# A value projection of 128x512 issued as two column halves of 128x256

## The chip, the core and the metric

The kernel runs on one core of a Trainium2 chip. The metric is device time in microseconds of one launch, as the median of several runs; beside it stands one execution that the hardware profiler recorded, with a span from its first to its last instruction. Engines are named as in the profile: PE is TensorE's matmul, PEld its weight load, DVE VectorE, ACT ScalarE, POOL GpSimd, SP the queue that issues most transfers.

## What is computed

The input x has 2048 rows of 512. A gate g = sigmoid(x . gate_w) mixes two branches per row:

```python
def _A_ref(x, wqkv, w_phi, wo):          # 32 heads of 16
    q, k, v = ...                        # x @ wqkv, split by head
    pq = einsum("bhsd,hdf->bhsf", q, w_phi)
    pk = einsum("bhsd,hdf->bhsf", k, w_phi)
    phi_q = concatenate([softmax(pq), softmax(-pq)], -1)
    phi_k = concatenate([softmax(pk), softmax(-pk)], -1)
    kv = einsum("bhsf,bhsd->bhfd", phi_k, v)
    z  = einsum("bhsf->bhf", phi_k)
    o = einsum("bhqf,bhfd->bhqd", phi_q, kv) / (einsum("bhqf,bhf->bhq", phi_q, z)[..., None] + 1e-6)
    return o @ wo
def _B_ref(x, w1, b1, w2, b2):           # 512 -> 1792 -> 512
    r = relu(x @ w1 + b1)
    return (r * r) @ w2 + b2
g = sigmoid((x * gate_w).sum(-1))
return g * A + (1 - g) * B
```

## The kernel before

**Precision.** Nearly every large product is made of three. A float32 array is split by `split` into a rounded part (type float32r, name ending in `h`) and a remainder (`l`). `mm3(o, a, b, sa, sb, first, last)` then adds high x high, high x low and low x high into the same PSUM tile. Its three lines are L69, L70 and L71 of the kernel before. Each matmul has a weight load of its own in the profile: the operand `a[:, sa]`, 128x128, is loaded into the array, and `b[:, sb]` is streamed through it.

**Tiling.** The rows are cut into 4 blocks of 512 (`NB`), each into 4 chunks of 128 (`NC`), so that there are 16 chunks. The 512 inputs are cut into 4 slices of 128 (`NK`).

**The branches.** The dense branch runs through a `work_list` of 2 sweeps x 4 blocks x 7 slices of the hidden layer: an "up" product (tile `u`, 12 matmuls of 128x512), ReLU and square on ACT, a split, and a "down" product into four PSUM tiles `d`. Two up products run ahead of the down products. The attention branch is laid over it by a table of slots: `at(slot, f, ...)` puts a step between two entries of the work list. For each chunk in the first sweep:

- `do_k` makes the keys' product `k` (a `project` of 12 matmuls) and its exponentials on DVE and ACT.
- `do_v` makes the values' product `v`, again `project(c, st["x", b], st["wb"], "v")`: the stationary operand is a slice of x, the streamed one the whole 512 columns of the split weights `wvh`, `wvl`. ACT then copies `v` out of PSUM into `vext`, which keeps a column of ones beside each head's 16 values.
- `do_kv`, for every second chunk, adds 2 x 32 small products of the exponentials with `vext` into `kvps`.

After the first sweep `kv_done` (DVE copies on L433, two transposes `kvt` on PE) lays the sums out, and the second sweep's slots hold the queries' products `q`, the numerators `num`, and the output projection `att`.

**Order.** The Tile framework turns the program text into one instruction stream per engine. It orders by priority, and `tc.high_priority(offset=AHEAD)` lifts a step ahead by `AHEAD` = 150 in program order. So more instructions in the text can move others. `k`, `v` and other short-lived products come from two one-bank pools by `bank(name)`. During the first sweep's attention work only one of these is in rotation, the other holds `kvps`.

The small matrices for the folded key and query weights (`fold`, L143) are float32 products, not float32r: tile `foldk`, 128x128.

Of the kernel before, what the change touches and what calls it, by code (L numbers as in the profile page):

```python
# [16 lines left out]
P = 128  # L17
S, D, H, DH, F = 2048, 512, 32, 16, 1792
NK = D // P
# [13 lines left out]
def tile_gated_mix(ctx: ExitStack, tc: tile.TileContext, xT, xn, wqT, wkT, wphi, wv, wo, w1, b1, w2, b2, gw, out):  # L33
    nc = tc.nc
# [16 lines left out]
    def bank(name):  # L51
        p = banks[taken[0] % len(banks)]
        taken[0] += 1
        return p.tile([P, 512], F32, tag="s", name=name)
# [11 lines left out]

    def mm3(o, a, b, sa, sb, first, last):
        (ah, al), (bh, bl) = a, b
        nc.tensor.matmul(o, ah[:, sa], bh[:, sb], start=first, stop=False)  # L69
        nc.tensor.matmul(o, ah[:, sa], bl[:, sb], start=False, stop=False)  # L70
        return nc.tensor.matmul(o, al[:, sa], bh[:, sb], start=False, stop=last)  # L71

    ALL = slice(0, 512)
    halves = (slice(0, 256), slice(256, 512))
# [7 lines left out]
    def row():  # L82
        return work.tile([P, D], F32, tag="row", name="row", bufs=6)
# [26 lines left out]
    st, up_w, down_w = {}, {}, {}  # L110
# [74 lines left out]
    def project(c, xs, ws, nm):  # L185
        ps = bank(nm)
        sc = slice(c * P, (c + 1) * P)
        for k in range(NK):
            mm3(ps, xs[k], ws[k], sc, ALL, k == 0, k == NK - 1)
        return ps  # L190
# [100 lines left out]
    def attended(o, u, wos):  # L291
        ps = bank("att")
        for r in range(2):
            for t in range(2):
                mm3(ps, o[r], wos[2 * r + t], slice((2 * t + u) * P, (2 * t + u + 1) * P), ALL,
                    r + t == 0, r + t == 2)
        return ps


    def up_step(ps, k, xs, wf):  # L300
        st["up"] = mm3(ps, wf, xs[k], slice(k * P, (k + 1) * P), ALL, k == 0, k == NK - 1)
# [104 lines left out]
        st["phi", n] = scaled(e3, r, nc.gpsimd)  # L406

    def do_v(b, n, c):
        ps = project(c, st["x", b], st["wb"], "v")
        with tc.high_priority(offset=AHEAD):  # L410
            nc.scalar.activation(heads(vext[n % NV])[:, :, :DH], ps.rearrange("p (h f) -> p h f", f=DH), AF.Copy)

# [68 lines left out]
    for b in range(NB):  # L481
        for c in range(NC):
            s = b * SL + 3 * c - 3 if b else 7 + c
            at(s, gate_load, b * NC + c)
            at(s + 3, gate_chunk, b * NC + c)
        at(b * SL + 4, do_x, b + 1)
        for c in range(NC):
            n = b * NC + c
            s = 5 + 2.9 * n
            at(s, do_k, b, c)  # L490
            at(s + 2, do_v, b, n, c)
            if c % 2:
                at(s + 5, do_kv, n - 1)
# [23 lines left out]
    hid, last = {}, len(work_list) - 1  # L517
# [19 lines left out]
    for t, (sw, b, i) in enumerate(work_list):  # L537
# [14 lines left out]
        for c in range(NC):  # L552
            n = b * NC + c
            done = ("f", n) in st
            if sw == 0:
                o = row()
                nc.scalar.activation(o, b2b, AF.Copy, scale=rest[:, n:n + 1])
            else:
# [3 lines left out]
                o = st["f", n]  # L562
# [53 lines left out]
```

## Time and profile before

| | |
|---|---|
| median of 3 runs | 531.95 us (530.74 to 532.16) |
| profiled execution, span | 528.2 us |
| around the span (median less span) | 3.75 us |
| PE busy | 519.0 us, 98% of the span, 3475 matmuls |
| PEld busy | 417.6 us, 79%, 3475 loads |
| DVE / ACT / POOL busy | 356.5 / 234.1 / 77.0 us |
| matmuls into `v` | 192, from 40.9 us to about 256 us |

For the profiled execution the profile gives the span and no other time. The 3.75 us are what the runs' median has beyond it. Matmul durations in the profile are modelled and overlap: a 128x512 product shows 389 ns, while the next one starts about 227 ns after it. What a product costs PE is therefore read from the distance of starts, not from its duration or from the busy sum.

### The profile page before, as it was taken

Reading aid. Unit: us, or ns where it says so; the run is one execution under the profiler, and the core shown is the slowest. Engines: PE = TensorE matmul, PEld = TensorE weight load, DVE = VectorE, ACT = ScalarE, POOL = GpSimd, SP = SyncE. Lnnn points to the kernel's source line nnn. Section 1 sums busy time; section 2 is a strip of 40 time slices with the busy share of each in tenths; the row PEclk is TensorE's granted clock in tenths of the full one; section 3 lists DMA queues with packets and bytes.
Section 4 is the critical chain, followed back from the end, with each engine's and each line's share of the span. In section 5 each row is a group of like instructions: output and inputs, shape, how many; then the busy total and the mean of one; then the engine's idle time right before and its main releaser. Section 6 shows DMA issues by size and latency. Waiting matters only on the chain.

```text
span 528.2 us, 8945 instructions
## 1 busy us (share of the span) xinstructions
PE 519.0 (98%) x3475; PEld 417.6 (79%) x3475; DVE 356.5 (68%) x608; ACT 234.1 (44%) x404; POOL 77.0 (15%) x61
## 2 busy tenths in 40 slices
PE   8998999999999999999999999999999999999997
PEld 4876888888888888888878878787887878787785
DVE  4688546833656334566769897998878887779423
ACT  4874424623335234354644663463435353535230
POOL 2001111111111111011103121102011111112000
PEclk9999999999999999999999999999999999999999
DMA  7974004200032000434346114134102311022102
GB/s 255 297 234 131 1 1 161 81 2 1 24 138 79 2 0 22 159 85 137 81 146 215 34 40 124 66 107 130 45 17 89 113 49 30 24 77 94 47 1 79
DMA packets 30834, 45.16 MB, mean 86 GB/s; under 512 B 5704, under 2 KB 12360, under 8 KB 30792
## 3 DMA queue, kind: packets, MB, share of 16 engines
q1 hardware_dynamic: 30328, 44.20, 26.8%
q8 instruction: 27, 0.44, 0.4%
q10 hardware_dynamic: 432, 0.39, 0.2%
q14 instruction: 15, 0.12, 0.1%
q0 software_dynamic: 32, 0.01, 0.0%
HBM read 29.89 MB, written 8.39 MB: 72 GB/s over the span
## 4 chain that ended last, share of the span: by engine, by line
PE 63%; DVE 15%; DMA 7%; ACT 5%; SPq 5%; issue 2%; POOL 2%; DVEq 0%; POOLq 0%; ACTq 0%
PE u L69 6%; PE u L71 6%; PE u L70 6%; PE d L71 6%; PE d L70 6%; PE d L69 6%; SPq L259 4%; PE k L69 3%; PE v L69 2%; PE k L70 2%; PE k L71 2%; PE v L70 2%; PE v L71 2%; DMA in<-in_w 2%; PE att L69 2%
## 5 line engine op out<-in xcount | busy, mean ns | idle before, releaser
L305 ACT ACTIVATE r<-u,b1c 128x512 f32<-128x512 f32 x56 | 38.5, 687 | 152.1 <-PE u L71 143.5
L69 PE MATMUL d<-w2h,hh 128*128 128x512 f32 x224 | 87.5, 390 | 0.0
L69 PE MATMUL u<-xh,w1h 128*128 128x512 f32 x220 | 86.8, 395 | 0.4 <-ACT w1h L61 0.4
L70 PE MATMUL d<-w2l,hh 128*128 128x512 f32 x224 | 87.2, 389 | 0.0
L71 PE MATMUL d<-w2h,hl 128*128 128x512 f32 x224 | 87.2, 389 | 0.0
L71 PE MATMUL u<-xh,w1l 128*128 128x512 f32 x220 | 85.8, 390 | 0.1
L70 PE MATMUL u<-xl,w1h 128*128 128x512 f32 x220 | 85.7, 390 | 0.0
L64 DVE TENSOR_TENSOR hl<-r,hh 128x512 fp32r<-128x512 f32 x56 | 42.8, 764 | 55.9 <-ACT hh L61 55.9
L233 POOL TENSOR_TENSOR ez<-e,z 128x512 f32<-128x512 f32 x32 | 41.4, 1316 | 187.7 <-ACT e L205 187.7
L214 POOL TENSOR_TENSOR e<-e,r 128x1024 f32<-128x1024 f32 x16 | 32.4, 2025 | 202.1 <-DVE r L210 144.8
L208 DVE TENSOR_REDUCE sm<-e 128x64 f32<-128x1024 f32 x32 | 39.0, 1217 | 28.5 <-ACT e L205 28.3
L69 PEld LDWEIGHTS u<-xh,w1h 128*128 128x128 f32 x220 | 41.3, 188 | 12.2 <-ACT hh L61 1.6
L71 PEld LDWEIGHTS d<-w2h,hl 128*128 128x128 f32 x224 | 42.1, 188 | 8.7
L69 PEld LDWEIGHTS d<-w2h,hh 128*128 128x128 f32 x224 | 42.0, 188 | 8.7
L70 PEld LDWEIGHTS d<-w2l,hh 128*128 128x128 f32 x224 | 42.1, 188 | 8.6
L71 PEld LDWEIGHTS u<-xh,w1l 128*128 128x128 f32 x220 | 41.3, 188 | 9.1 <-DVE w1l L64 0.6
L70 PEld LDWEIGHTS u<-xl,w1h 128*128 128x128 f32 x220 | 41.3, 188 | 8.2
L205 ACT ACTIVATE e<-e 128x1024 f32<-128x1024 f32 x32 | 33.8, 1055 | 23.2 <-DVE e L203 22.4
L257 ACT ACTIVATE phiT<-tb 32x256 f32<-32x256 f32 x64 | 26.4, 413 | 34.6 <-DVE tb L251 33.9
L61 ACT ACTIVATE hh<-r 128x512 fp32r<-128x512 f32 x56 | 35.2, 628 | 1.3
L306 ACT ACTIVATE r<-r 128x512 f32<-128x512 f32 x56 | 35.1, 627 | 1.0
L566 DVE SCALAR_TENSOR_TENSOR row<-d,rest,row 128x512 f32<-128x512 f32 (+1 forms) x33 | 22.4, 731 | 8.5 <-PE d L71 8.5
(106 smaller groups left out, 875.4 us busy)
## 6 DMA issues: line engine op xcount, KB each, us to landing
in<-in_xT SPq DMA_DIRECT2D x32, 256.0 KB, 3.8
in<-in_w SPq DMA_DIRECT2D x24, 256.0 KB, 3.1
phiT<-tb SPq DMA_DIRECT2D x192, 32.0 KB, 1.8
row<-in_xn SPq DMA_DIRECT2D x16, 256.0 KB, 2.8
part<-row SPq DMA_DIRECT2D x16, 256.0 KB, 2.0
row<-part SPq DMA_DIRECT2D x16, 256.0 KB, 3.7
out<-row SPq DMA_DIRECT2D x15, 256.0 KB, 2.3
row<-in_wkT SPq DMA_DIRECT2D x4, 256.0 KB, 5.8
```

Of the source, the lines that this page charges most:

```text
L61: i = nc.scalar.activation(hi, src, AF.Copy)
L64: elo.tensor_tensor(lo, src, hi.bitcast(F32), ALU.subtract)
L69: nc.tensor.matmul(o, ah[:, sa], bh[:, sb], start=first, stop=False)
L70: nc.tensor.matmul(o, ah[:, sa], bl[:, sb], start=False, stop=False)
L71: return nc.tensor.matmul(o, al[:, sa], bh[:, sb], start=False, stop=last)
L205: nc.scalar.activation(ef, ef, AF.Exp)
L208: nc.vector.tensor_reduce(sm, e3, AX.X, ALU.add)
L214: eng.tensor_tensor(e3, e3, w.unsqueeze(2).to_broadcast([P, 2 * H, DH]), ALU.mult)
L233: nc.gpsimd.tensor_tensor(ez[:, hs, :], e3[:, hs, :], zbc[half], ALU.mult)
L257: nc.scalar.activation(dst, src, AF.Copy)
L305: nc.scalar.activation(r, ps, AF.Relu, bias=b1c[:, fc:fc + 1])
L306: nc.scalar.activation(r, r, AF.Square)
```

## The change

The values' product of a chunk is no longer one group of 12 matmuls over 512 columns. It is two groups of 12 over 256 columns each, one after the other, into the two halves of the same PSUM tile. `start` is set only on the first matmul of the first half, `stop` on the last slice of each half. The stationary slices of x are the same in both halves, and are loaded once for each matmul as before. ACT's copy of `v` still follows the whole tile. `skip_group_check` is an argument of the build and not an instruction.

```diff
     def mm3(o, a, b, sa, sb, first, last):
         (ah, al), (bh, bl) = a, b
-        nc.tensor.matmul(o, ah[:, sa], bh[:, sb], start=first, stop=False)
-        nc.tensor.matmul(o, ah[:, sa], bl[:, sb], start=False, stop=False)
-        return nc.tensor.matmul(o, al[:, sa], bh[:, sb], start=False, stop=last)
+        skip = o.shape[-1] < 512
+        nc.tensor.matmul(o, ah[:, sa], bh[:, sb], start=first, stop=False, skip_group_check=skip)
+        nc.tensor.matmul(o, ah[:, sa], bl[:, sb], start=False, stop=False, skip_group_check=skip)
+        return nc.tensor.matmul(o, al[:, sa], bh[:, sb], start=False, stop=last, skip_group_check=skip)
...
     def do_v(b, n, c):
-        ps = project(c, st["x", b], st["wb"], "v")
+        ps = bank("v")
+        sc = slice(c * P, (c + 1) * P)
+        for h in halves:
+            for k in range(NK):
+                mm3(ps[:, h], st["x", b][k], st["wb"][k], sc, h, k == 0 and h is halves[0], k == NK - 1)
```

`halves` is `(slice(0, 256), slice(256, 512))`. The two instruction streams differ as follows. First, on PE at the first values' product, before: the last slices of `v`, and then the down products `d`.

```order
L69 MATMUL v<-wvh_293,xh_2_164 128x512
L70 MATMUL v<-wvl_294,xh_2_164 128x512
L71 MATMUL v<-wvh_293,xl_2_165 128x512
L69 MATMUL v<-wvh_299,xh_3_173 128x512
L70 MATMUL v<-wvl_300,xh_3_173 128x512
L71 MATMUL v<-wvh_299,xl_3_174 128x512
L69 MATMUL d_303<-w2h_245,hh 128x512
```

The same place on PE after the change: the end of the first half and the beginning of the second.

```order
L70 MATMUL v<-wvh_293,xh_2_164 128x256
L71 MATMUL v<-wvl_294,xh_2_164 128x256
L72 MATMUL v<-wvh_293,xl_2_165 128x256
L70 MATMUL v<-wvh_299,xh_3_173 128x256
L71 MATMUL v<-wvl_300,xh_3_173 128x256
L72 MATMUL v<-wvh_299,xl_3_174 128x256
L70 MATMUL v<-wvh_281,xh_0_136 128x256
L71 MATMUL v<-wvl_282,xh_0_136 128x256
L72 MATMUL v<-wvh_281,xl_0_137 128x256
```

All four slices of x are gone through twice; the 16 places hold 384 matmuls of 128x256 where there were 192 of 128x512. Apart from these, one matmul changes its place on PE. It is the first of an up product near the end of the first sweep, where `kvt` transposes the summed values. The piece of the difference, by names without numbers of buffers and lines:

```diff
 MATMUL d<-w2h,hl 128x512
-MATMUL u<-xh,w1h 128x512
 MATMUL kvt<-ident,row 128x128 x2
 MATMUL q<-wqh,xh 128x512
 ...
 MATMUL q<-wqh,xl 128x512
+MATMUL u<-xh,w1h 128x512
 MATMUL u<-xl,w1h 128x512
```

It moves from ahead of the two transposes to behind the twelve query products. On ACT one pair changes places, a little earlier. Before, the ReLU stands ahead of the third split of the output weights:

```order
L411 ACTIVATE vext_108<-v 128x32x16
L61 ACTIVATE wqh_2603<-foldq_2598 128x512
L305 ACTIVATE r<-u,b1c 128x512
L61 ACTIVATE woh_2795<-in 128x512
L61 ACTIVATE wqh_2651<-foldq_2646 128x512
```

On ACT after the change, the split comes first:

```order
L416 ACTIVATE vext_108<-v 128x32x16
L61 ACTIVATE wqh_2795<-foldq_2790 128x512
L61 ACTIVATE woh_2987<-in 128x512
L306 ACTIVATE r<-u,b1c 128x512
L61 ACTIVATE wqh_2843<-foldq_2838 128x512
```

The ReLU now stands behind a split that waits for transfers of `wo`. On DVE one small `rest<-gate` operation of 128x1 moves ahead of four others; POOL and SP keep their order.

## The prediction

> **What bounds the kernel now.** I read the page's busy shares first, then PE's waits, then the starts of single matmuls in the timeline.
>
> ```profile
> span 528.2 us, 8945 instructions
> PE 519.0 (98%) x3475; PEld 417.6 (79%) x3475; DVE 356.5 (68%) x608; ACT 234.1 (44%) x404; POOL 77.0 (15%) x61
> PEclk9999999999999999999999999999999999999999
> ```
>
> PE has work for 98% of the span, at the full granted clock in every slice. A busy share of overlapping matmuls proves little, so the waits of PE come next: who it waited for, total us, times, longest.
>
> ```profile
> PE warm L360 <- DVE zeros L354: 1.2, 1, 1.2
> PE k L69 <- ACT vext L411: 1.1, 1, 1.1
> PE num L270 <- DMA phiT<-tb: 1.1, 2, 0.6
> PE u L69 <- ACT w1h L61: 0.4, 1, 0.4
> PE kvt L444 <- DVE row L433: 0.4, 1, 0.4
> PE v L69 <- DVE e L203: 0.3, 1, 0.3
> PE foldk L143 <- DVE wkl L64: 0.2, 1, 0.2
> ```
>
> All seven together make 4.7 us. So the span is the sum of what PE's instructions cost each other in distance, and a change of that distance goes into the time nearly whole. No slack in PE can swallow more than a part of the 1.4 us that `k` and `v` wait in the table above. The values' products are 192 in the stretch from 40 to 256 us (a window of the tile `v` alone; PE's busy time and count come first after the length):
>
> ```profile
> 40.00:256.00 216.00, 47.13 (x192) 35.35 (x192) 9.15 (x16) 1.00 0.20 62
> ```
>
> What one of them costs is seen in the timeline of PE at a values' product in the middle (start, duration):
>
> ```profile
> 154.16 0.50 PE L69 MATMUL v<-wvh,xh 128*128 128x512 f32 x1
> 154.50 0.40 PE L70 MATMUL v<-wvl,xh 128*128 128x512 f32 x1
> 154.74 0.39 PE L71 MATMUL v<-wvh,xl 128*128 128x512 f32 x1
> ...
> 157.01 0.39 PE L69 MATMUL u<-xh,w1h 128*128 128x512 f32 x1
> ```
>
> From 154.74, the third of twelve, to 157.01, where the next group starts, there are ten distances: 2.27 us, or 0.227 us each. The shown duration of 0.39 is latency. The 192 products thus cost 192 x 0.227 = 43.6 us. The first distance is longer, 0.34 us, and the weight loads of the same place say why:
>
> ```profile
> 154.16 0.19 PEld L69 LDWEIGHTS v<-wvh,xh 128*128 128x128 f32 x1
> 154.27 0.19 PEld L70 LDWEIGHTS v<-wvl,xh 128*128 128x128 f32 x1
> 154.50 0.19 PEld L71 LDWEIGHTS v<-wvh,xl 128*128 128x128 f32 x1
> ```
>
> After the small products the first load has nothing to hide behind. 0.34 - 0.227 = 0.11 us is the price of a bare load, which the next load's start, 0.11 later, confirms. In the steady run a load starts with the product before it and is done long before 0.227 is over. This is the margin that a half-width product uses up.
>
> **The change part by part.** Removed: 192 products of 512 columns. Added: 384 of 256 columns with 384 loads of 128x128 in place of 192. The columns streamed are the same in number. What remains is whether a half-width product follows after half of 0.227, that is 0.1133 us, or later. No float32r product of 256 columns is in the trace, so I bound it.
>
> From below: the float32 products of the folded weights, on full 128x128 weights of the same size, with a load each. The timeline shows sixteen in a row, and the tile's summary their duration:
>
> ```profile
> 22.46 1.95 PE L143 MATMUL foldk<-row 128*128 128x128 f32 x16
> ...
> L143 PE MATMUL foldk<-row x32: 270/275/377, 22.5 to 29.4; 128*128 128x128 f32 x32
> ```
>
> (1.95 - 0.275) / 15 = 0.1117 us each. Two rows of other widths tell that a float32 column costs about two of float32r:
>
> ```profile
> L270 PE MATMUL num<-phiT,kvb 64*32 64x256 f32 x256 | 10.6, 382 | 1.2 <-DMA phiT<-tb 1.1
> L223 PE MATMUL kvps<-e,vext 128*17 128x32 f32 x1024 | 10.3, 197 | 0.0
> ```
>
> (382 - 197) / (256 - 32) = 0.83 ns of latency per column, against 0.227 / 512 = 0.44 ns per float32r column. So 128 float32 columns are about as much streaming as 256 here, and the load is equal. This is the nearest row: 384 x (0.1117 - 0.1133) = -0.6 us.
>
> Toward the expensive side: a part of the 0.227 may be paid per product and not per column. The warm-up products at the start, also 512 columns, show it. Their first and last regular loads, nine rows:
>
> ```profile
> 1.60 0.15 PEld L360 LDWEIGHTS <-zeros 128*128 128x128 bf16 x1 [0.27 <-issue]
> ...
> 5.01 0.15 PEld L360 LDWEIGHTS <-zeros 128*128 128x128 bf16 x1 [0.27 <-issue]
> ```
>
> 3.41 / 8 = 0.426 us each, 1.88 times 0.227. If the array runs at half speed there (my assumption, since the granted clock's row shows 9 from the first slice), then streaming 512 columns at full speed takes 0.213 us, and 0.0137 us of the 0.227 are a fixed part. A half-width product then costs 0.1065 + 0.0137 = 0.120 us, and 384 x 0.120 - 192 x 0.227 = +2.6 us. The load, 0.11, still fits under 0.120, but only just.
>
> The Trainium skill, TensorE: Matmul & The Clock Gate, section Back-to-back issue gap, gives the distance as columns / 1.2 ns when cold and columns / 2.4 + 2.5 ns when warm. The cold figure, 427 ns, agrees with 0.426; the warm one, 216 ns, does not agree with 0.227, so 11 ns here are not in that formula. By the page's fixed part alone the sum would be 192 x 2.5 ns = +0.5 us.
>
> The upper bound: the load cannot begin before the fixed part is over. Then a half-width product costs 0.111 + 0.0137 = 0.1247 us, and the sum is 384 x 0.1247 - 43.6 = +4.3 us. I take 0.120: the warm-up and the float32r products are 512 columns on full weights both, while the fold has the slower float32 columns, in whose pauses a fixed part can hide.
>
> The moved up product. It stood in a gap that PE has anyway:
>
> ```profile
> 270.32 0.39 PE L71 MATMUL d<-w2h,hl 128*128 128x512 f32 x1
> 270.55 0.39 PE L69 MATMUL u<-xh,w1h 128*128 128x512 f32 x1
> 271.33 0.41 PE L444 MATMUL kvt<-ident,row 128*128 128x128 f32 x2 [0.40 <-DVE row L433]
> ```
>
> `kvt` waits for DVE's copies, whose chain hangs on the last `kvps` and is not moved against PE. With the up product behind the query products, PE waits 0.227 us longer there and pays the product later: +0.2 us, its whole price, from nothing to 0.23.
>
> The swapped ReLU on ACT:
>
> ```profile
> 259.23 0.69 ACT L305 ACTIVATE r<-u,b1c 128x512 f32<-128x512 f32 x1 [1.02 <-PE u L71]
> 259.81 0.62 ACT L61 ACTIVATE woh<-in 128x512 fp32r<-128x512 f32 x1
> ...
> 267.69 0.50 PE L69 MATMUL d<-w2h,hh 128*128 128x512 f32 x1
> ```
>
> Before the ReLU ACT sat idle for 1.02 us, in which the split can run if its data has come; if not, the hidden tile is late by 0.6 us or somewhat more. The down product that uses such a tile runs at 267.69, eight microseconds on. I cost it at nothing; without that cover it would be 0.6. `vext` is copied as before, after the whole of `v`, and who waits for it moves with it. The sum: +2.6 + 0.2 = +2.8 us on the profiled 528.2, and the same on the median, which lies 3.75 above that span: 531.95 + 2.8 = 534.8.
>
> **The rivals.** *Half the columns, half the time.* The 0.227 is all per column, or the fixed part is small; the fold's pace speaks for it, the 1.88 of the warm-up against it. Price -0.6 to +0.5 us, with the moved product 531.5 to 532.7: not slower. It decides from the distance of two starts inside `v`: a slowdown over 0.3% (1.6 us, about what a measurement here can tell from no change) less the 0.2 needs 0.1133 + 1.4 / 384 = 0.117 us or more. The page's formula lies inside this rival. Chance 0.26.
>
> *The load becomes the limit.* A load, the swap and then the product, each waiting for the other: 0.1247 us, 531.95 + 4.3 + 0.2 = 536.5. For it: a bare load costs 0.11, as much as a half's streaming. Against it: the fold runs loads of the same size at 0.1117. Chance 0.10.
>
> *Nothing of the load is hidden, or the float32r rate is lost at 256 columns.* With bare loads 192 more of 0.11 cost +21 us: 553. At the pace of float32, 0.83 ns per column, 256 columns cost 0.21 and the sum is +37 us: 569. The steady 0.227 against the bare 0.34 speaks against the first; nothing in the trace against the second but that width plays no part in any row. Together 0.02. The same page, section The mechanism of Part 3, says that a load overlaps running products only where its rows of the array differ; by that rule the steady distance before would be 0.34, and the trace refutes it.
>
> *Faster by over 0.3%.* 384 products would have to follow at 0.109 or less, below the quickest row, or the order's small moves save a wait: 0.04. That the change does nothing is excluded by the streams, which hold 384 products of 128x256.
>
> **How the numbers follow.** Fixed part: 0.58, 534.8. Load-limited 0.10 and the two dear cases 0.02, all slower: 0.70. Halved cost 0.26, all within 0.3%. Faster 0.04. The range goes from the halved case at the fold's pace, 531.5, less 0.4 for the runs' spread, 531.1, to the load-limited one, 536.5, and 0.7 (half the 1.4 us between the runs before) above it, 537.2. It leaves out the dear cases and most of the faster one.
>
> **What would show it.** In the timeline of the changed kernel the starts inside `v` stand 0.120 us apart if I am right, 0.112 to 0.114 if halving is free, 0.125 if the load limits; each 0.01 is 3.8 us. Starts of `u` and `d` stay at 0.227. PE's busy sum would rise whatever happens, since durations overlap more, and proves nothing. `kvt` should wait 0.6 in place of 0.4. A new large wait of PE for `vext`, or for hidden tiles about 265 us, would make my covers wrong; distances of 0.117 or less, or the order's moves costing over 1 us, the forecast.

## The result, and the profile after

The changed kernel takes 535.5 us (median of 3 runs, 534.44 to 536.0) against 531.95: ratio 1.0073, 95% interval 1.0045 to 1.0101. That is slower by 2.4 to 5.4 us. The forecast was 534.8 in a range of 531.1 to 537.2.

The profiled execution is 533.7 us long, 5.5 us more than that of before. These are the page's first lines for the changed kernel, and the two rows of its queues that matter below:

```profile
span 533.7 us, 9329 instructions
PE 522.4 (98%) x3667; PEld 428.4 (80%) x3667; DVE 357.0 (67%) x608; ACT 233.8 (44%) x404; POOL 76.6 (14%) x61
...
q1 hardware_dynamic: 30328, 44.20, 26.2%
q8 instruction: 29, 0.48, 0.4%
```

There are 192 more matmuls and 192 more weight loads. Queue q1 moves the same 44.20 MB, but the instruction queue has 29 packets where before it had 27. Inside `v`, PE's timeline (start, duration) reads:

```profile
155.21 0.39 PE L70 MATMUL v<-wvh,xh 128*128 128x256 f32 x1
155.43 0.28 PE L71 MATMUL v<-wvl,xh 128*128 128x256 f32 x1
155.55 0.29 PE L72 MATMUL v<-wvh,xl 128*128 128x256 f32 x1
...
158.06 0.28 PE L72 MATMUL v<-wvh,xl 128*128 128x256 f32 x1
158.18 0.40 PE L70 MATMUL u<-xh,w1h 128*128 128x512 f32 x1
```

From the second product, at 155.43, to the next group, at 158.18, there are 23 distances: 2.75 us, 0.1196 us each. The first distance is longer by a bare load, as before: 0.22 in place of 0.12.

PE's waits (total us, times, longest) and the row of the transposes show what the forecast had and what it did not have:

```profile
PE num L271 <- DMA phiT<-tb: 2.5, 2, 1.6
...
PE k L70 <- ACT vext L416: 0.9, 1, 0.9
...
PE kvt L449 <- DVE row L438: 0.6, 1, 0.6
...
273.49 0.41 PE L449 MATMUL kvt<-ident,row 128*128 128x128 f32 x2 [0.59 <-DVE row L438]
```

`kvt` waits 0.6 in place of 0.4, as forecast. But the numerators, which need the transposed `phiT`, wait 2.5 us in place of 1.1. Behind the last of these waits PE ran slowly for a while:

```profile
507.10 0.63 PE L71 MATMUL u<-xl,w1h 128*128 128x512 f32 x1
507.52 0.63 PE L72 MATMUL u<-xh,w1l 128*128 128x512 f32 x1
507.95 0.63 PE L70 MATMUL u<-xh,w1h 128*128 128x512 f32 x1
```

These up products stand 0.42 to 0.43 us apart, not 0.227. Windows show the granted clock (the number after PE's, PEld's, DVE's, ACT's and POOL's times), 0.84 over 11 us there and 1.00 at the like place before:

```profile
500.00:511.00 11.00, 9.39 (x60) 6.48 (x59) 2.30 (x4) 1.28 (x3) 0.00 (x0) 0.84 0.08 22
```

From 506 to 509 us alone it is 0.50.

So the loss in this execution has three parts. By the transposes `kvt`, which start at 273.49 in place of 271.33, 2.2 us are lost. The moved up product then adds 0.2. About 3 us come from the numerators' waits (1.4 us longer than before) and the slow stretch (0.16 x 11 = 1.8 us). The experiments ask whether the last part is chance, and if not, what it is.

### The profile page after: what moved, and what is told of

Same layout as the page of the kernel before. It is cut to its first block, busy times and chain, and to the rows that moved or that the text cites. A ratio compares the mean times of both kernels' runs of the same rounds, so it can differ in the third digit from the quotient of the medians.

```text
span 533.7 us, 9329 instructions
## 1 busy us (share of the span) xinstructions
PE 522.4 (98%) x3667; PEld 428.4 (80%) x3667; DVE 357.0 (67%) x608; ACT 233.8 (44%) x404; POOL 76.6 (14%) x61
## 3 DMA queue, kind: packets, MB, share of 16 engines
q1 hardware_dynamic: 30328, 44.20, 26.2%
## 4 chain that ended last, share of the span: by engine, by line
PE 71%; DVE 11%; SPq 6%; DMA 4%; ACT 4%; POOL 2%; issue 2%; DVEq 0%; ACTq 0%; POOLq 0%
PE u L70 7%; PE d L71 7%; PE d L72 7%; PE u L72 7%; PE d L70 7%; PE u L71 7%; SPq L260 5%; PE v L70 3%; PE v L72 3%; PE v L71 3%; PE k L70 3%; PE k L71 3%; PE k L72 3%; PE att L70 2%; POOL ez L234 2%; PE att L71 2%
## 5 line engine op out<-in xcount | busy, mean ns | idle before, releaser
L64 DVE TENSOR_TENSOR hl<-r,hh 128x512 fp32r<-128x512 f32 x56 | 41.4, 739 | 57.9 <-ACT hh L61 57.9
L70 PE MATMUL v<-wvh,xh 128*128 128x256 f32 x128 | 37.0, 289 | 0.5 <-DVE e L204 0.5
L72 PE MATMUL v<-wvh,xl 128*128 128x256 f32 x128 | 36.3, 283 | 0.0
L71 PE MATMUL v<-wvl,xh 128*128 128x256 f32 x128 | 36.3, 283 | 0.0
```

What stands on the lines that cost most here:

```text
L64: elo.tensor_tensor(lo, src, hi.bitcast(F32), ALU.subtract)
```

## Experiments

**The kernel before, again.** No edit.

> The kernel before, unchanged, against itself. It tells how far its profile's waits vary: the changed kernel's profile has, beside starts 0.120 us apart inside v, a wait of the last numerators for phiT of 1.6 us (0.6 before) and up products 0.43 apart behind it, at a lower granted clock; together some 2.5 us that are not in the forecast. Theory A (the extra at the end is chance, and belongs to both kernels): here too some executions have the long wait and the slow up products; ratio 1.000, within 0.2%; spans spread by 1 to 2.5 us. Theory B (the change lengthens that wait): the last wait for phiT stays at about 0.6 us here, the tail keeps full clock, spans agree within 0.5 us.

Ratio 1.0008 (0.9998 to 1.0017); spans of single executions from 528.9 to 530.9, a spread of 2.0 us, as theory A had it. But the long wait that theory A expected is not in the one execution that was profiled. The wait for `phiT` is the one known from before:

```profile
PE num L270 <- DMA phiT<-tb: 1.1, 2, 0.6
```

It also shows that an execution takes 1.8 us more than its span (531.97 and 530.2 here). The 528.2 that the prediction was worked out on was thus a quick execution, and the 3.75 us "around the span" were half that.

**The changed kernel, again.** No edit.

> The changed kernel again, in more rounds. Theory A: the lasting part is the 384 products at 0.120 us (+2.6) and the moved up product (+0.2), so the ratio settles near 1.0053 (1.004 to 1.0065), and the tail's wait and clock differ from execution to execution. Theory B (the tail's wait belongs to the change): ratio 1.007 to 1.010, with a long last wait for phiT and a slow stretch of PE behind it again.

536.69 us, ratio 1.0111 (1.0093 to 1.013), above the ranges of both theories. Theory A falls: the extra belongs to the change. The waits for `phiT` are long again, 1.7 at the last numerators, and 2.2 at the first, which the profile puts down to ACT:

```profile
PE num L271 <- ACT xh L61: 2.2, 1, 2.2
PE num L271 <- DMA phiT<-tb: 1.7, 1, 1.7
```

**The moved up product alone.** On the kernel before:

```diff
+            if "q_first" in st and k == 0:
+                with tc.issue_after(st.pop("q_first").ins):
+                    up_step(ps, k, xs, wf)
...
+            if "q_down" in st:
+                held.enter_context(tc.issue_after(st["q_down"].ins))
```

Both names hold the last matmul of the first query product, so that neither an up nor a down product slips in ahead of it. But for the width of `v`, PE's order is then that of the changed kernel. The pairs exchanged on ACT and DVE stay as before.

> The kernel before with whole 512-column values' products, and on PE exactly the order of the changed kernel: the first matmul of one up product stands behind the first twelve query products instead of ahead of kvt. Theory A: kvt waits 0.6 us instead of 0.4, all else alike: +0.2 us, ratio 1.0004 (0.999 to 1.002). Theory B in the form that the moved order delays the queries' chain and so the numerators: a wait for phiT longer by 0.5 to 1.5 us, ratio 1.002 to 1.005.

530.89 us, ratio 1.0 (0.999 to 1.0009). `kvt` waits 0.6 and the numerators 1.1:

```profile
PE num L273 <- DMA phiT<-tb: 1.1, 2, 0.6
...
PE kvt L457 <- DVE row L446: 0.6, 1, 0.6
```

PE's order is not what lengthens the numerators' waits. What is left of the change is the number and width of PE's instructions and the pairs exchanged on ACT and DVE, so I followed the transfers that the numerators wait for.

**What is late at the last numerators.** Each pair of chunks needs 24 small transfers `phiT<-tb`, issued one after another by SP. SP's timeline for the last pair, from four profiles (before, before again, the changed kernel, the changed kernel again), each row with its start and length:

```profile
484.62 15.08 SPq L259 DMA_DIRECT2D phiT<-tb  x24
```

```profile
486.64 15.07 SPq L259 DMA_DIRECT2D phiT<-tb  x24
```

```profile
487.55 16.07 SPq L260 DMA_DIRECT2D phiT<-tb  x24
```

```profile
489.75 16.17 SPq L260 DMA_DIRECT2D phiT<-tb  x24
```

A median issue takes 0.589 us. The changed kernel's train of issues is 1.0 to 1.1 us longer, and all of it is in one issue:

```profile
490.64 1.58 SPq L260 DMA_DIRECT2D phiT<-tb  x1
```

In a window from 490.4 to 492.4 us of the same kernel, the queues show what else moved then (packets, MB, share of the 16 engines):

```profile
q1 hardware_dynamic: 96, 0.07, 13.4%
q8 instruction: 1, 0.02, 3.5%
```

One packet of instructions, 16 KB. Over the train of before, from 484.62 to 499.7, there is none:

```profile
q1 hardware_dynamic: 1056, 0.72, 17.9%
```

The same holds for the first pair's train: one instruction packet from 296.5 to 311.7 in the changed kernel, none from 294.1 to 309.3 before. So theory P: a block of program loaded while SP issues makes that issue about 1 us longer. Its rival Q: the half-width products or the order lengthen the waits themselves. The kernel before was spared at the two trains for which PE waits, and the added instructions moved later blocks onto them. The Trainium skill, Runtime: NRT & Kernel Launch, section Instruction fetch mechanics, says that each engine's program is refilled in blocks of 16 KiB, 256 instructions, by a DMA queue of its own. The 16 KB packets agree. By the Trainium skill's 256 instructions in a block, 384 added instructions are an estimated one and a half blocks, so the phase moves by half a block. The same section of the Trainium skill calls the cost of a block's boundary mostly hidden. Here it is not hidden where the packet meets an issue of SP: that issue is 1 us longer.

**The changed kernel with the program's phase moved.**

```diff
-        idle(11)
+        idle(9)
+        for i in range(52):
+            j = 32 * (i % 4)
+            nc.tensor.matmul(st["warm"][j:j + 32, :32], st["zeros"][:, j:j + 32], st["zeros"][:, :32],
+                             start=True, stop=True, skip_group_check=True)
```

Two of the eleven warm-up products give way to 52 tiny ones, which makes 50 pairs of load and matmul more. The profile shows two moves beside that, both near the start: one matmul of an up product stands eight places later on PE, and one pair on ACT changes places.

> The changed kernel with 50 more pairs of load and matmul at the very start: 2 of the 11 warm-up products are replaced by 52 tiny ones of 32x32. All else, products and order, is the same. Theory P (phase of PE's instruction loads): the 384 additional PE instructions of the change moved the later loads of PE's program onto SP's phiT issues (loads at 305.8 and 490.7 us in the changed kernel's profile, inside the trains of issues at 296.5 and 487.6), each making one issue 0.4 to 1.1 us longer; 50 pairs move these loads about 11 us earlier, to about 294 and 480, ahead of both trains. Expected: the waits of num for phiT back at about 1.1 us in total, no slow stretch of PE in the tail, and 2 to 2.7 us faster than the changed kernel: ratio to the kernel before 1.004 to 1.0065. Rival Q (the longer waits come from the 256-column products or the moved order themselves): waits of 2.5 to 3.9 us stay, ratio 1.009 to 1.013.

532.69 us, ratio 1.0041 (1.0024 to 1.0059). The numerators wait 1.1 us again, and the last train has 24 issues in 15.07 us, as in the kernel before (15.08 and 15.07):

```profile
PE num L271 <- DMA phiT<-tb: 1.1, 2, 0.6
```

```profile
488.30 15.07 SPq L260 DMA_DIRECT2D phiT<-tb  x24
```

The two packets now come at 295.4 and 486.1 us, ahead of the trains that start at 297.7 and 488.3; the second moved by 4.6 us only, not by the 11 that I expected. All 384 half-width products, the moved product and the exchanged pairs on ACT and DVE are still there, so none of them makes the long waits. P has what it asked for, Q has not.

**The same addition on the kernel before.** The same edit, with the same small moves near the start.

> The kernel before, 512 columns and old order, with the same 50 additional pairs at the start. Theory P: its loads of PE's program, at 288.9 and 480.8 us before and 312.5 and 502.4 behind the two trains of phiT issues (294.1 to 309, 484.6 to 499.7), move about 11 us earlier, so that those behind land inside both trains, near 301 and 491. Expected: the waits of num for phiT grow from 1.1 to 2.5 to 3.5 us and the kernel is slower by 1 to 2.7 us: ratio 1.002 to 1.005. Rival Q: no change, ratio 1.000 within 0.1%, waits stay at 1.1.

530.49 us, ratio 1.0005 (0.9989 to 1.002). On the total P missed: I expected 1.002 to 1.005. Only one of the two trains was hit, the last:

```profile
PE num L270 <- DMA phiT<-tb: 1.8, 2, 1.3
```

```profile
484.00 15.80 SPq L259 DMA_DIRECT2D phiT<-tb  x24
```

```profile
q8 instruction: 1, 0.02, 0.4%
```

(The last row is the window from 484 to 499.8 us.) The train is 0.7 us longer with one instruction packet in it, and PE's last wait grew from 0.6 to 1.3. The first train had none: the block there moved by 1.5 us only, not by the 11 that I had reckoned, so 50 pairs do not move all blocks alike. The 0.7 us were offset in this profile by as much at the beginning, where waits for the first transfers differ from one execution to the next. Within the interval the total shows nothing, so this run carries the mechanism in its trace and not in its time.

**Both side by side.** The changed kernel and its shifted form had run on different chips so far, so both ran on one chip:

> The changed kernel once more, on the same chip and in the same call as the shifted one (e10), since the two were compared on different chips before. Theory P: instruction loads again inside the trains of phiT issues, waits of num at 2.5 to 3.9 us, ratio 1.009 to 1.012. If the chip made the difference, this comes out near e10, at 1.004 to 1.006.

> The changed kernel with the 50 additional pairs at the start, beside e9. Theory P: waits of num at 1.1 us, ratio 1.004 to 1.006, 2 to 3.5 us under e9. If the chip made the difference, both have the same ratio within 0.2%.

The changed kernel: 534.8 us, ratio 1.0077 (1.0055 to 1.0099). The shifted one: 532.39 us, ratio 1.0027 (1.0016 to 1.0038). Both ratios lie below the ranges expected for them, 1.009 to 1.012 and 1.004 to 1.006. Their difference, 2.4 us, is within the 2 to 3.5 expected. The intervals do not touch, so it is not the chip. The waits and the last train, first of the changed kernel and then of the shifted one:

```profile
PE num L271 <- DMA phiT<-tb: 2.7, 2, 1.8
...
489.38 16.25 SPq L260 DMA_DIRECT2D phiT<-tb  x24
```

```profile
PE num L271 <- DMA phiT<-tb: 1.0, 2, 0.6
...
486.88 15.07 SPq L260 DMA_DIRECT2D phiT<-tb  x24
```

The waits make 1.7 of the 2.4 us. The rest is not shown to come from the packets: the two profiles also differ ahead of the first `v`, which starts at 42.6 and at 40.7 us. This start varies from 40.3 to 42.9 among all ten profiles of the table below, so it may be chance, or the work of the altered warm-up.

**All profiles side by side.** Two stretches of PE's timeline leave that beginning out: from the first to the last start in `v`, and from the start of `kvt` to the end of the span. The table includes the kernel with paired halves, which is described below.

| kernels | `v` | `kvt` to the end | waits of `num` |
|---|---|---|---|
| before; again; order alone | 214.4; 214.4; 214.5 | 256.9; 256.9; 257.1 | 1.1 each |
| changed and shifted; beside | 216.6; 216.7 | 257.1; 257.1 | 1.1; 1.0 |
| before, shifted (one train hit) | 214.3 | 257.7 | 1.8 |
| changed; again; beside; paired halves (both trains hit) | 216.8; 217.0; 216.9; 216.7 | 260.2; 260.0; 258.8; 258.9 | 2.5; 3.9; 2.7; 2.8 |

So `v` costs 2.1 to 2.7 us more wherever it is cut in halves, the moved product 0.2, and the hit trains 1.6 to 3.1 more in the second stretch. Of these ten profiles' twenty trains that PE waits for, nine hold an instruction packet, and each of the nine has one issue of 1.0 to 1.8 us. In the other eleven no issue is longer than 0.65. In the changed kernel run again the first numerators go on 2.1 us behind the end of their train, in its other profiles 1.4; what made these 0.8 us (2.14 less 1.38) is open.

**What sets the distance of 0.120 us.** Three kernels vary the pieces of `v`.

Four pieces of 128 columns (`h = slice(128 * i, 128 * i + 128)` for four `i`):

> The values' products in four pieces of 128 columns: 768 matmuls. If the fixed part of 0.0137 us per product is all there is, starts inside v are 0.053 + 0.0137 = 0.067 us apart and the whole costs 51.5 us against 43.6: +8 us, about 540. If a weight load of 0.11 us per product must fit between two starts, they are 0.111 to 0.114 apart, 85 to 88 us: +42 to +44 us, about 575. If load and fixed part add, 0.125 apart and +52 us.

589.32 us in one run. The timeline, from the second product of a group on:

```profile
154.77 0.27 PE L71 MATMUL v<-wvl,xh 128*128 128x128 f32 x1
...
156.67 0.28 PE L70 MATMUL v<-wvh,xh 128*128 128x128 f32 x1
```

17 distances in 1.90 us, 0.1118 each: the weight load sets the pace, as with the folds' 0.1117. `v` costs 768 x 0.1118 - 192 x 0.227 = +42 us, as the second theory said. The rest of the 58 is in waits and in the clock: `k` waits 11.0 us for ACT's `vext`, which I did not expect and did not follow up, and the mean granted clock was 0.991, which over 587.5 us is an estimated 5 us at most.

Pieces of 384 and of 128 columns (`for h in (slice(0, 384), slice(384, 512))`):

> The values' products in pieces of 384 and of 128 columns. With a fixed part of 0.0137 us per product, starts inside the wide piece are 0.160 + 0.0137 = 0.1737 us apart; if the 0.227 were all per column, 0.170. Inside the narrow piece the load sets 0.111 to 0.112, as with four pieces of 128. A pair then costs 0.285 in place of 0.240 for halves: +11 us against the kernel before in v.

551.26 us in one run. A wide piece, then a narrow one:

```profile
180.76 0.33 PE L70 MATMUL v<-wvh,xh 128*128 128x384 f32 x1
...
181.63 0.33 PE L72 MATMUL v<-wvh,xl 128*128 128x384 f32 x1
...
181.86 0.27 PE L71 MATMUL v<-wvl,xh 128*128 128x128 f32 x1
...
182.98 0.28 PE L72 MATMUL v<-wvh,xl 128*128 128x128 f32 x1
```

0.87 / 5 = 0.174 and 1.12 / 10 = 0.112. For `v` that makes 192 x 0.286 - 43.6 = +11 us. The total rose by 20.6, with further waits of `v`, `k` and `num` and a mean granted clock of 0.993.

The two halves of each slice next to each other (loop over `k` outside, over `h` inside):

> Halves as in the changed kernel, but the two halves of one slice follow each other, so that within a slice the order of the stationary operands is high, high, low, high, high, low. If the fixed part belongs to changing the weights and a load of the same weights is free, some of the starts come closer than 0.120 us (0.107 to 0.110); if each product pays for its own load whatever it holds, all stand at 0.120.

534.86 us in one run, 4.2 above the kernel before beside it. Two of its rows, with 21 distances between them:

```profile
156.38 0.28 PE L72 MATMUL v<-wvh,xl 128*128 128x256 f32 x1
...
158.90 0.28 PE L72 MATMUL v<-wvh,xl 128*128 128x256 f32 x1
```

2.52 / 21 = 0.120. That the loads of a slice come closer to each other brings nothing. In every kernel the second product of three has the same weights as the first, and it follows at the same distance as the others.

Together: 0.112 at 128 columns, 0.120 at 256, 0.174 at 384, 0.227 at 512. From 256 on this is a line: (0.227 - 0.120) / 256 = 0.42 ns per column and 0.013 us per product. At 128 columns this line would give 0.067; the measured 0.112 is the price of a bare load, so there the load is the floor.

## Why the prediction was right, and where not

*The half-width product.* Right, in the mechanism too: 0.120 forecast, 0.1196 measured. The fixed part came from the warm-up products at half pace, 0.0137 (0.014 by the rounded figures shown); the line through three widths gives 0.013. The half pace was an assumption. It is borne out from 506 to 509 us of the first profile: at a granted clock of 0.50, products of 512 columns stand 0.42 to 0.43 apart, like the warm-up's 0.426. For the warm-up itself the profile shows no lower clock. The fold's row was read wrongly. 128 columns of float32r stand 0.112 apart as well, so the fold's 0.1117 is the pace of the load and says nothing of the price of 256 columns.

*The sum in `v`.* 384 x 0.1196 - 192 x 0.227 = +2.3 us, against the forecast 2.6; the stretch of `v` is 2.1 to 2.7 us longer in the table. Nearly all of the forecast is here. The shifted kernel, which has little else left, is 0.27% (1.4 us, 0.8 to 2.0) slower in one comparison and 0.41% (2.2 us, 1.3 to 3.1) in the other. The first is below the 2.5 us of `v` and the moved product, so the shift may itself save some tenths of a us at the beginning; this was not separated.

*The moved product.* `kvt` waits 0.6 in place of 0.4, as forecast, and the trace shows its 0.2 us (257.1 in place of 256.9 in the table). In the time of the kernel with the order alone it is too small to be told from nothing (interval 0.999 to 1.0009).

*The ReLU and `vext`.* Rightly costed at nothing: `k` waits 0.9 us for `vext`, 1.1 before.

*The rivals.* Half the time for half the columns is refuted by 0.1196; the load as the limit holds at 128 columns (0.112), not at 256; no product lost its rate.

*What the sum lacked.* A term for what additional instructions do off PE. I counted 384 matmuls and loads on PE's own path, but not the blocks of program that they need. In the plain changed kernel this term is about as large as the one I forecast: 2.4 us between the two medians on one chip, 1.6 to 3.1 us in the profiles. So that the total of 2.8 came close to the result of 3.5 is in part luck. The terms that the traces show add up to about 4 us and more. The first comparison, of 3 runs each, came out low: its kernel before took 531.95, and 531.2, 530.65 and 531.12 in the three later ones. In the two further comparisons the plain kernel was 1.0077 and 1.0111 times the kernel before, that is +4 to +6 us, and the intervals of both lie above a rise of 2.8 us. My list of what would prove me wrong named waits for `vext` and hidden tiles, and not the numerators, though their row stood among the seven waits that I quoted.

*Open.* The drop of PE's clock behind the last numerators was seen in the first profile of the changed kernel, and not at that place in e9's. It followed a wait of 1.6 us, yet e9 waited 1.8; what decides it was not tried. It is no single case. A drop of this size takes the mean granted clock of an execution to 0.996. The mean is 0.997 or less in 6 of 15 executions of the plain changed kernel, in 2 of 12 of the one with one train hit, and in 2 of 93 of the kernels whose profiles show both trains spared. Four of the 6 are among the six executions of e2, which may be why its ratio is the highest. So part of what the long waits cost may be paid in clock; where in those executions it dropped, no profile shows. That a program block delays an issue is shown by place and size in the trains above, and by moving it. By what path it does so, no run shows, nor why some packets fall into a train and lengthen no issue, as one at 433.7 us in the kernel before.

## What to carry to other kernels

Where a matrix engine is the bound, read a product's cost from the distance of starts at two widths and split it into a part per column and a part per product; splitting a product costs the second part once more, and a weight load sets a floor. An edit that adds instructions also moves where the program is loaded: before a few us are put down to the edit itself, shift the phase with cheap instructions at the start, look whether the packets did move off, and see what stays. Queues that issue many small transfers in a row ahead of a waiting engine are the places to look at.

## What the runs showed of the hardware

- Consecutive float32r products with a load of 128x128 each cost 0.42 ns per streamed column and 0.013 us per product from 256 to 512 columns; at 128 columns 0.112 us, as much as a bare load.
- A 16 KB packet on the instruction queue during SP's issue of a small transfer made that issue 1.58 us long in place of 0.589; the other issues hit in the trains ahead of the numerators took 1.0 to 1.8. With these packets moved off the trains by instructions added at the start, the changed kernel was 2.4 us faster on one chip, with waits for these transfers 1.7 us shorter in the profiled executions.
- PE at a granted clock of 0.50 from 506 to 509 us (0.84 over 11 us), with products of 512 columns 0.42 to 0.43 us apart, behind a wait of 1.6 us.
